# A gated mix of a state-space layer and linear attention: a new step list, and the last two output rows scaled and stored in halves

## Chip, cores and metric

The kernel runs on one core of a Trainium2 chip. The metric is the device time of one execution in microseconds. The profile is that of one further execution, taken by the hardware profiler; its span is the time from the first to the last instruction of the program on the core.

## What is computed

The input `x` has 2048 rows of 512 numbers. Branch `a` is a diagonal state-space layer (512 complex states, a recurrence over the rows), branch `b` is linear attention with 32 heads of 16, whose features are pairs of softmaxes. A gate of one number per row mixes them. Cut to what matters:

```python
g = sigmoid((x * gate_w).sum(-1, keepdims=True))
# a: h = Lam_bar * h + B_bar x_t, row by row;  y = 2 Re(C h) + x * Dskip
# b: q, k, v = x @ wqkv; phi = [softmax(+-(q|k) @ w_phi)]
#    kv = sum_s phi_k v;  z = sum_s phi_k;  o = phi_q kv / (phi_q z + 1e-6);  b = o @ wo
return g * a + (1 - g) * b
```

## The kernel before, in words

The 2048 rows are taken in 8 residues r of the row number modulo 8 and two halves each: 16 tiles of 128 rows. The recurrence over 2048 rows becomes one over 256 blocks (a scan on VectorE) and matmuls between residues. Nothing loops at run time: the order of all work on TensorE (PE), VectorE (DVE), ScalarE (ACT) and SyncE (SP) is a list written out by hand, the string `ORDER` (line 24). Each word names a step, a Python generator, and each time that the word occurs the step emits its next part. An engine executes its own parts in the order in which the list gives them. Behind `@` stand the numbers of the PSUM banks that the step takes; it has to wait until whoever had them has been read out. `:D` gives an evacuation or a scaling to VectorE instead of ScalarE, `:A` gives an output store to ScalarE's DMA queue instead of SyncE's. `F:28` puts 28 filler matmuls.

The steps that matter here, with the names of their tiles in the profile:

- `l8` to `l15` (`st_l`): SyncE loads one 128-row tile of x, transposed by the DMA, into `xT`; the tiles 0 to 7 are loaded ahead of the list. `NR`, `NI` load the real and imaginary part of B (512 KB each) into `Bn`.
- `k`, `v`, `q` (four matmuls of 512 columns each, line 475, and an evacuation): projections of one tile of x. `k9` needs x tile 9.
- `g`, `h`, `z`, `c`: the state-space branch. `y`: its output for one tile (`py`; two groups of four 512-column matmuls at line 717, then four 128-column matmuls with the diagonal of Dskip at line 722).
- `x`, `n`, `e`, `s` and, for the queries, `X1`-`X3`, `N1`-`N3`, `E1`-`E3`, `S1`-`S3`: softmax features of groups of four tiles. X and N are trees of maxima and minima on VectorE (line 511), then a subtraction; E is four exponentials on ScalarE; S is a tree of sums on VectorE, a logarithm on ScalarE, a difference on VectorE (line 553), an exponential on ScalarE, a multiplication on VectorE (line 559), and then four transposes by DMA, issued by SyncE (line 563), into `phT`. S1 gives the tiles of o4 to o7, S2 those of o8 to o11, S3 those of o12 to o15.
- `o0` to `o15` (`st_o`): attention output of one tile. Two matmul groups into `pn` (line 736), each followed by a logarithm and a copy to `nu`; then an exponential `rd`, a multiplication `on` (line 744), and a transpose into `oT`: by DMA from SyncE for the first twelve, by TensorE (`po`, line 753) for o12 to o15.
- `t0` to `t15` (`st_t`, line 761): four matmuls with `Wo` into the same `py` (line 765), then the scaling by the gate into `ot` (line 769 on ScalarE, 771 on VectorE), then one store of 128 rows of 512 numbers to the output (line 773).

The list ends with t15, t13 and t14.

Of the kernel before, what the change touches and what calls it, by code (L numbers as in the profile page):

```python
# [23 lines left out]
ORDER = """
NR F:28 NI B W1@0 W0@1 W0 W2@2 W1:D W3@3 W3 f1@4 W2:D f0@5 f2@6 f0 f1:D l10 V@0 F:4 V P f3@1 f3 f2:D F:4 P P k1@2 k1
l13 P2 k0@3 P2 U P2 P2 P2 P2 P4 k2@4 P3 P3 k3@5 P4 P4 k0 v0@0 i0 i2 U i0 i0 i1 i2 k4@7 i0:D i0 k2 i2 i2:D i2 U k3 k5@6
i1 v3@1 n0 x0 l9 i1 V2@2 i3 l12 x0 k4 v2@3 i3 i3 l14 i1 k5 n0 x0 n0 x0 i3 k7@4 n0 x0 U n0 i1 l11 k6@5 n1 x1 x1 n1 x1
n1 l8 R0 R1 x1 i3 k7 M v7@7 x1 n1 n1 k6:D L V2 v1@6 x2 n2 e0 v6@4 v5@5 v4@2 e0 x2 s0 v0 l15 n2 s0 n2 v2 s0 v1 R2 s0 v6
v3 n2 k10@0 k10 s0 k9@3 k9 C4 k13@6 gw D R3 s0 k12@4 e1 v7 s0 e1 s1 C6 k11@1 k11 x2 s1 k14@0 k8@3 k12 k14 k8 v4 k13
a0@71 a0 x2 s1 x2 s1 v5 g00@4 g00 g60@0 n2 x3 s1 g20@3 g60 s1 g10@2 g10 n3 e2 g30@6 g40@5 g10 s1 a1 x3 g20 n3 a1 x3 n3  # L30
x3 g41@4 n3 C3 e2 e2 e2 x3 g30 g40 g30 k15@0 k15 n3 e3 s2 x4 s2 x4 g01@2 g01 e3 e3 s2 g50@3 g11@5 g50 s2 s2 s2 n4 x4
n4 Q3 n4 s2 g50 g21@6 e3 s3 v8@0 g31@2 g11 Q2 g11 n4 g70@3 Q1 s3 C7 g21 g70 v9@5 g70 g70 z0 z0 g31 g31 Q0 w1@6 C0 a2
a2 a2 w0@3 s3 z0 v11@2 v9 g61@5 g41 R4 z0 w1 v8 z0 z0 g61 s3 w2@4 s3 s3 a2 x4 z0 z0 g51@6 g51 x4 w2 C2 s3 w3@0 g51 v11
n4 R5 w3 g71@5 g71 g71 g71 z1 z1 g02@4 g02 g42@6 a3 a3 z0 z0 g42 w0 e4 e4 z1 z1 z1 g62@2 g12@0 q1@5 C1 h50@4 C5 J1 e4
e4 z1 q2@6 q2 g12 g12 g22@3 g22 J0 h50 z1 z1 g62 q3@4 q3 J2 s4 z1 s4 q0@6 z1 s4 q0 q1 xA nA g32@0 J3 g32 g32 h60@3 J0
g52@2 g52 c4 h60 J2 c4 g52 h51@4 c2 s4 s4 g72@6 R7 g72 xA h10@5 nA g72 g72 c2 xA J3 nA h10 v10@0 v10 J1 s4 c5 h51 c5
R6 g23@3 v12@2 c4 c0 c0 g63@5 nA z2 z2 a3 a3 g03@4 xA g03 z2 z2 z2 z2 xA g23 z2 z2 g33@6 c5 v12 z2 z2 g13@0 g13 g63
g43@4 h32@3 g13 nA g43 h52@2 h52 g33 h32 h61@5 h61 h12@0 c0 g53@4 h12 g33 g53 s4 v14@3 c2 eA eA h42@2 h42 g73@6 g53 eA
eA g73 g73 q10@5 sA h11@0 h11 O h00@4 g73 sA v13@2 h00 v13 a4 z3 sA v15@6 z3 v15 h20@0 h01@4 h30@2 v14 h20 sA h30 z3
h31@6 z3 z3 sA a4 h01 h31 c6 c6 sA q13@3 q13 z3 a4 a4 Y Y h22@0 G q10 z3 z3 G q6@2 q6 h22 z3 z3 sA sA Y Y c1 c1 q9@4  # L40
q8@6 q5@7 h62@3 h41@5 c3 h41 c1 c3 c3 h13@0 h62 q11@2 h13 q11 q8 q12@1 c6 q12 h21@5 q5 h21 h02@2 c7 q4@6 q4 h53@3 h53
h23@1 h23 h33@0 h33 sA q9 h40@7 h40 sA q7@5 h43@6 h63@3 c7 h43 q7 c7 y4@0 y4 sA h63 sA h03@1 END h02 o0@4 o0 X1 N1
o1@7 o1 q14@6 X1 N1 h03 o0@5 X1 o1@2 o1 o1 o0 o0 q15@3 o2@4 o2 o2@7 o2 N1 q15 X1 N1 X1 N1 E1 E1 y2@1 y1@2 y1 E1 E1 q14
# [25 lines left out]
def kernel(  # L69
# [691 lines left out]
    def st_t(n):  # L761
        ti = order[n]
        py, oT = live["py", n], live["oT", n]
        for g in range(HG):
            MM(out=py[:], lhsT=oT[:, g, :], rhs=Wo[:, g, :], start=False, stop=(g == HG - 1))  # L765
        yield
        ot = pools["op"][1].tile([P, D], BF16, name="ot", bufs=14)
        if sel["eng"] == "act":
            nc.scalar.mul(out=ot[:], in_=py[:], mul=G[:, ti:ti + 1])  # L769
        else:  # L770
            VS(out=ot[:], in0=py[:], scalar1=G[:, ti:ti + 1], scalar2=None, op0=ALU.mult)
        yield
        sel["q"].dma_start(out=out_par[:, ti // 2, ti % 2, :], in_=ot[:])
        yield
# [73 lines left out]
```

## Time and profile before

| | |
|---|---|
| median of three runs | 155.21 us (154.76 to 155.4) |
| profiled execution's own time | 155.28 us |
| its span | 153.2 us |
| granted TensorE clock, mean | 0.995 |
| instructions | 3361 |

The profile's engines: PE is TensorE's matmuls, PEld its weight loads, DVE VectorE, ACT ScalarE, POOL GpSimd, SP SyncE; a q behind a name means the sequencer that issues DMAs or waits. A row of a timeline gives the start, the duration, the engine, the line, the operation, the tiles as out<-in, the shape and how many instructions are merged in it; in brackets the idle time of the engine before it and what ended it. Durations of neighbouring instructions of one engine overlap, so what one costs its engine is the distance from its start to the next one's start. "Chain" is the work that ended last, followed back from the end.

### The profile page before, as it was taken

The page shows a single profiled execution, that of the slowest core. Times are in us where ns is not written, and L with a number is a line of the kernel's source. Part 1 is how long each engine was busy: PE and PEld are TensorE (multiplying, and loading weights), DVE is VectorE, ACT ScalarE, POOL GpSimd, SP SyncE. Part 2 cuts the span into 40 slices and gives each one's busy share as a digit, 9 for nine tenths or more (in the row PEclk, how much of TensorE's full clock was granted, in tenths as well). Part 3 has the DMA queues.
Part 4 walks back from the last instruction along what each step waited for, and adds up shares of the span by engine and source line. Part 5 has one row for each costly group of instructions (what it writes and reads, how often), then busy time and mean ns, then how long its engine had stood idle before and what let it go on. Part 6 is the DMA issues. An engine that isn't in the chain of part 4 may idle for free.

```text
span 153.2 us, 3361 instructions
## 1 busy us (share of the span) xinstructions
PE 146.2 (95%) x1236; PEld 95.0 (62%) x1254; DVE 132.4 (86%) x303; ACT 129.2 (84%) x279; POOL 15.8 (10%) x43
## 2 busy tenths in 40 slices
...
GB/s 116 164 218 97 223 178 112 103 75 103 103 107 78 129 230 178 166 115 4 0 0 4 0 0 169 74 37 34 42 98 147 176 122 189 162 129 206 247 143 103
DMA packets 50848, 17.55 MB, mean 115 GB/s; under 512 B 44176, under 2 KB 50832, under 8 KB 50832
## 3 DMA queue, kind: packets, MB, share of 16 engines
...
q8 instruction: 10, 0.16, 0.5%
q0 software_dynamic: 160, 0.01, 0.2%
q14 instruction: 6, 0.05, 0.1%
...
## 4 chain that ended last, share of the span: by engine, by line
PE 78%; SPq 10%; DMA 7%; issue 1%; ACT 1%
PE pgq L601 18%; PE py L717 16%; PE pq L475 9%; PE py L765 8%; SPq L229 8%; PE pv L475 4%; PE ph L668 4%; PE pk L475 4%; DMA xT<-in_A_x_dram 4%; PE kvacc L578 3%; DMA phT<-EEq 3%; PE pn L736 3%; PE pgq L606 2%; PE py L722 2%; PE pgq L608 2%; SPq L284 1%
## 5 line engine op out<-in xcount | busy, mean ns | idle before, releaser
L601 PE MATMUL pgq<-xT,BT 128*128 128x256 bf16 x256 | 31.5, 272 | 0.0
L475 PEld LDWEIGHTS <-xT 128*128 128x128 bf16 x192 | 18.2, 98 | 18.3 <-DMA xT<-in_A_x_dram 0.7
L601 PEld LDWEIGHTS <-BT 128*128 128x128 bf16 x256 | 24.6, 98 | 4.1
L138 ACT ACTIVATE EEk<-EEk 128x1024 bf16<-128x1024 bf16 x20 | 20.4, 1080 | 0.0
L119 ACT CAST uv<-pgq 128x512 bf16<-128x512 f32 x28 | 15.9, 605 | 0.5 <-PE pgq L601 0.4
L475 PE MATMUL pv<-Wv,xT 128*128 128x512 bf16 x59 | 15.5, 379 | 0.3
L475 PE MATMUL pq<-Wq,xT 128*128 128x512 bf16 x60 | 15.4, 379 | 0.2
L765 PE MATMUL py<-Wo,oT 128*128 128x512 bf16 x62 | 15.3, 379 | 0.1
L475 PE MATMUL pk<-Wk,xT 128*128 128x512 bf16 x62 | 14.7, 379 | 0.3 <-DMA xT<-in_A_x_dram 0.2
L138 ACT ACTIVATE EEq<-EEq 128x1024 bf16<-128x1024 bf16 x12 | 11.7, 1042 | 0.3 <-DVE EEq L527 0.3
L769 ACT ACTIVATE ot<-py,G 128x512 bf16<-128x512 f32 x12 | 7.9, 686 | 4.5 <-PE py L765 4.3
L138 ACT ACTIVATE ld<-pn 128x16 f32<-128x16 f32 x32 | 6.1, 191 | 5.7 <-PE pn L736 4.6
L590 ACT ACTIVATE phT<-X,dgB 128x512 bf16<-128x512 bf16 x16 | 10.7, 725 | 0.0
L119 ACT CAST nu<-pn 128x256 bf16<-128x256 f32 x27 | 9.9, 380 | 0.0
L119 ACT CAST vx<-pv 128x512 bf16<-128x512 f32 x16 | 9.1, 604 | 0.4 <-PE pv L475 0.4
L548 DVE TENSOR_TENSOR EEk<-EEk,rck 128x4096 bf16<-128x4096 bf16 (+1 forms) x5 | 9.3, 1858 | 0.0
L744 DVE TENSOR_TENSOR on<-nu,rd 128x512 bf16<-128x512 bf16 x16 | 6.7, 421 | 2.8 <-ACT rd L138 1.6
L765 PEld LDWEIGHTS <-oT 128*128 128x128 bf16 x64 | 5.7, 97 | 5.3 <-DMA oT<-on 0.5
L119 ACT CAST Xq<-pq 128x512 bf16<-128x512 f32 x16 | 8.9, 608 | 0.0
L119 ACT CAST Xq<-pk 128x512 bf16<-128x512 f32 x15 | 8.6, 598 | 0.4 <-PE pk L475 0.4
L736 PEld LDWEIGHTS <-phT 128*128 128x128 bf16 x128 | 6.2, 97 | 3.8 <-DMA phT<-EEq 1.4
L511 DVE TENSOR_TENSOR smk<-smk 128x512 bf16<-128x512 bf16 (+4 forms) x18 | 8.1, 448 | 0.1
...
## 6 DMA issues: line engine op xcount, KB each, us to landing
...
out_dram<-ot ACTq DMA_DIRECT2D x8, 128.0 KB, 2.5
out_dram<-ot SPq DMA_DIRECT2D x8, 128.0 KB, 2.2
...
```

What stands on the lines that cost most here:

```text
L119: nc.scalar.copy(out=out_ap, in_=in_ap)
L138: ins = nc.scalar.activation(**kw)
L229: nc.sync.dma_start_transpose(out=xT[:, :, ti * P:(ti + 1) * P], in_=x_res[ti // 2, ti % 2])
L475: MM(out=pt[:], lhsT=xT[:, kt, ti * P:(ti + 1) * P], rhs=W[:, kt, :], start=(kt == 0), stop=(kt == KT - 1))
L511: VT(out=dst, in0=cur[:, :, :, 0:n, :], in1=cur[:, :, :, n:2 * n, :], op=op)
L548: VT(out=E5, in0=E5, in1=rc.to_broadcast([P, L, 2 * NB, Dh, 4]), op=ALU.mult)
L590: nc.scalar.mul(out=t_, in_=x_, mul=c_)
L601: MM(out=pg[:, h, :], lhsT=BT[:, kt, 2 * j + h, :], rhs=xT[:, kt, r * NC:(r + 1) * NC], start=(h == 0 and kt == 0), stop=(r % 2 == 0 and k ...
L717: MM(out=py[:], lhsT=hs(r, t, slice(a * P, (a + 1) * P)), rhs=C2B[t], start=(t == 0), stop=False)
L736: MM(out=pn[:, 4 * m:4 * m + 4, :].rearrange("p h e -> p (h e)"), lhsT=ph[:, 4 * hf + m, :], rhs=KVm[:, 4 * hf + m, :], start=(m == 0), st ...
L765: MM(out=py[:], lhsT=oT[:, g, :], rhs=Wo[:, g, :], start=False, stop=(g == HG - 1))
L769: nc.scalar.mul(out=ot[:], in_=py[:], mul=G[:, ti:ti + 1])
```

## The change

The list is replaced by another with the same 855 words. All steps do the same work, with other neighbours, other PSUM banks and other marks. At the head l14 and NI come ahead of l9 and NR; the K and V projections up to k15 come in another order. In the middle the state-space and attention steps are interleaved anew. At the end the last three rows are t15, t13, t14 again.

In `st_t`, for n of 14 and 15, the scaled row tile is made in two tiles `oh0` and `oh1` of 256 columns each, the left half scaled by ScalarE, the right half by VectorE, and each half is stored by itself, the left from ScalarE's queue, the right from SyncE's. The diff, with the list cut to its head, the stretch from S1 to E3 and its tail:

```diff
-NR F:28 NI B W1@0 W0@1 W0 W2@2 W1:D W3@3 W3 f1@4 W2:D f0@5 f2@6 f0 f1:D l10 V@0 F:4 V P f3@1 f3 f2:D F:4 P P k1@2 k1
-l13 P2 k0@3 P2 U P2 P2 P2 P2 P4 k2@4 P3 P3 k3@5 P4 P4 k0 v0@0 i0 i2 U i0 i0 i1 i2 k4@7 i0:D i0 k2 i2 i2:D i2 U k3 k5@6
-i1 v3@1 n0 x0 l9 i1 V2@2 i3 l12 x0 k4 v2@3 i3 i3 l14 i1 k5 n0 x0 n0 x0 i3 k7@4 n0 x0 U n0 i1 l11 k6@5 n1 x1 x1 n1 x1
...
-X2 y0@5 y0 o1 y4 X2 N2 X2 o0 o0 o3@4 o3 o3@7 o3 o1 o3 y2 X2 N2 o2 X2 N2 S1 S1 N2 S1 o3 S1 N2 S1 S1 o3 y5@3 o2 o2 S1 S1
-S1 y1 E2 E2 E2 E2 y9@6 G N3 y5 y5 y3@4 y2 X3 X3 N3 t1 G t1 N3 S1 N3 S2 y9 y9 S2 S2 S1 S1 S2 y3 y3 t3 y0 t0 t0 t2 t2
-y6@7 X3 t2:A o4@2 o4 o4@5 o4 o4 y6 y6 t3 X3 o4 X3 o4 S2 S2 t3 o5@1 o5 o5@2 o5 o5 y13@5 y13 o5 N3 o6@4 S2 o6 o6@1 o6 o6
-y12@2 o5 y7@4 y7 y12 o6 o6 t4 y7 S2 S2 t4:D S2 E3 E3 E3 E3 S2 o7@1 o7 t5 t5 S3 o7@0 o7 S3 o7 t6 S3 o7 S2 o7 y8@1 o8@3
...
-o11 y15 o13@4 o13:D o13@6 t6:A o13 o13 o11 o12 y10@1 o14@4 y15 o14:D o12@6 t9 o12:D t7:A t1 y10 y10 o13 o15@4 o15
-o15@6 t4:A t5 o15 o15 t8 o15 t12 t12 t12:A t10 o14@4 o14 o14 t10:D o13@6 t11 o15@2 o15 t10 o13:D t11 t11:A y13 t13 o14
-o14@1 t15 t15 t15 o14:D t14 t13 t13 t14 t14:A
+B l14 NI l9 NR F:28 W1@0 W1 W0@1 W0:D l8 W2@2 W2:D W3@3 W3 f1@4 f1:D f0@5 f0 f2@6 V@0 V P f2:D F:4 U P U l11 P2 P2 P2
+f3@1 P2 P2 P4 U f3 F:4 P4 P k1@2 P4 V2@3 V2 k1 l10 P2 P3 i1 P3 i2 k0@4 k0 i1 k2@5 k3@0 i3 i1 i1:D i1 v0@7 l13 k4@6 i2
+i2 l12 i3 i3 k3 v4@1 x0 k2 x0 i2 i0 x0 k4 n0 i0 i0 i0 R0 k5@2 k5 x0 n0 v1@3 i3:D i3 k6@4 x0 n0 x1 R1 n0 i2 x1 R2 i0 L
...
+E1 X2 N2 y0@4 y0 X2 G N2 X2 o1 X2 S1 N2 q15@1 S1 o3@7 o3 o3@5 o1 q15 o2 N2 o3 S1 o3 o3 S1 y1@3 N2 S1 S1 S1 X3 S1 E2 E2
+E2 y6 y6 o3 E2 S1 S1 y3 X3 N3 G X3 G y4@2 y4 y9@7 X3 y2@1 y9 y2 y2 y1 t2 y0 N3 y1 t1 S1 t0 t3 t0 t1 t3 X3 S2 y5@5 y5
+N3 t2 S2 S2 N3 S2 S1 o4@4 o4 o4@3 y13@6 o4 o4 o4 t3:A y4 o5@1 o5 o5@4 o5 o5 N3 S2 o5 y5 y7@3 o6@1 o6 t2 o6@4 o6:D y13
+o4 o6 y12@1 o5 S2 S2 o6 y12 y7 E3 E3 E3 o6 S2 S2 S2 o7@4 S2 t4 t5 S2 o7 o7@4 y7 t4:D E3 t0:A S3 S3 S3 t6 y12 o7 o7 o7
...
+t7:A o12@2 o12 o12@3 o12 o12 o12 y15 o13@7 o13 o13@2 o13:D o13 t6 y11 y10@3 y15 o14@7 o14 o12@2 o12:D y10 t5:A o15@7
+t8:A o15 o15@2 o15:D o15 o15 t12 o13 t12 t12 o14@7 o14 o14 o14 y10 t10 o15@2 t10 o13@1 o13 t11 o14@7 t11 o14 o15:D t11
+t10:A t15 t15 t15 t13 t13 t13 t14 t14 t14
...
             MM(out=py[:], lhsT=oT[:, g, :], rhs=Wo[:, g, :], start=False, stop=(g == HG - 1))
         yield
+        if n >= NTI - 2:
+            ha = [pools["op"][1].tile([P, D // 2], BF16, name=f"oh{c}", bufs=2) for c in range(2)]
+            nc.scalar.mul(out=ha[0][:], in_=py[:, 0:D // 2], mul=G[:, ti:ti + 1])
+            VS(out=ha[1][:], in0=py[:, D // 2:D], scalar1=G[:, ti:ti + 1], scalar2=None, op0=ALU.mult)
+            yield
+            for c, q in enumerate((nc.scalar, nc.sync)):
+                q.dma_start(out=out_par[:, ti // 2, ti % 2, c * (D // 2):(c + 1) * (D // 2)], in_=ha[c][:])
+            yield
+            return
         ot = pools["op"][1].tile([P, D], BF16, name="ot", bufs=14)
```

More of the change, by code (lines that the diff above doesn't have):

```diff
@@ L24 @@
 ORDER = """
-NR F:28 NI B W1@0 W0@1 W0 W2@2 W1:D W3@3 W3 f1@4 W2:D f0@5 f2@6 f0 f1:D l10 V@0 F:4 V P f3@1 f3 f2:D F:4 P P k1@2 k1
-l13 P2 k0@3 P2 U P2 P2 P2 P2 P4 k2@4 P3 P3 k3@5 P4 P4 k0 v0@0 i0 i2 U i0 i0 i1 i2 k4@7 i0:D i0 k2 i2 i2:D i2 U k3 k5@6
-i1 v3@1 n0 x0 l9 i1 V2@2 i3 l12 x0 k4 v2@3 i3 i3 l14 i1 k5 n0 x0 n0 x0 i3 k7@4 n0 x0 U n0 i1 l11 k6@5 n1 x1 x1 n1 x1
-n1 l8 R0 R1 x1 i3 k7 M v7@7 x1 n1 n1 k6:D L V2 v1@6 x2 n2 e0 v6@4 v5@5 v4@2 e0 x2 s0 v0 l15 n2 s0 n2 v2 s0 v1 R2 s0 v6
-v3 n2 k10@0 k10 s0 k9@3 k9 C4 k13@6 gw D R3 s0 k12@4 e1 v7 s0 e1 s1 C6 k11@1 k11 x2 s1 k14@0 k8@3 k12 k14 k8 v4 k13
@@ L30 @@
[L30 to L43, printed above, removed]
-X2 y0@5 y0 o1 y4 X2 N2 X2 o0 o0 o3@4 o3 o3@7 o3 o1 o3 y2 X2 N2 o2 X2 N2 S1 S1 N2 S1 o3 S1 N2 S1 S1 o3 y5@3 o2 o2 S1 S1
@@ L45 @@
-S1 y1 E2 E2 E2 E2 y9@6 G N3 y5 y5 y3@4 y2 X3 X3 N3 t1 G t1 N3 S1 N3 S2 y9 y9 S2 S2 S1 S1 S2 y3 y3 t3 y0 t0 t0 t2 t2
-y6@7 X3 t2:A o4@2 o4 o4@5 o4 o4 y6 y6 t3 X3 o4 X3 o4 S2 S2 t3 o5@1 o5 o5@2 o5 o5 y13@5 y13 o5 N3 o6@4 S2 o6 o6@1 o6 o6
-y12@2 o5 y7@4 y7 y12 o6 o6 t4 y7 S2 S2 t4:D S2 E3 E3 E3 E3 S2 o7@1 o7 t5 t5 S3 o7@0 o7 S3 o7 t6 S3 o7 S2 o7 y8@1 o8@3
-t6 o8 o8@0 o8 o8 S3 S3 y12 t0:A y11@7 o8 o8 o9@3 o9:D o9@0 o9:D S3 y8 y8 o9 o9 S3 S3 o9 o10@3 y11 o10 o10@0 y11 o10
-o10 S3 y14@3 S3 y14 t7 t7:D t8 y14 t8 y15@0 o11@4 S3 o11 o11@1 t9 o12@4 o11:D o11 S3 o10 o10 o12 o12@1 o12 o12 t9:D
@@ new lines @@
+i2 l12 i3 i3 k3 v4@1 x0 k2 x0 i2 i0 x0 k4 n0 i0 i0 i0 R0 k5@2 k5 x0 n0 v1@3 i3:D i3 k6@4 x0 n0 x1 R1 n0 i2 x1 R2 i0 L
+n0 x1 n1 n1 gw C0 l15 x1 R3 k6:D k7@0 k7 n1 U n1 x1 n1 e0 e0 k14@5 x2 n2 s0 v3@6 k14 x2 s0 v6@2 v6 k9@4 k9 v7@0 v0 v7
+v3 x2 v5@5 s0 n2 s0 s0 v5 n2 M D v2@2 s0 s0 v2 k8@4 e1 e1 s1 v1 k8 k11@7 k13@0 x2 k10@6 k10 s1 n2 k12@5 k12 a0@23 a0
+k13 s1 k11 g40@4 g40 x2 s1 s1 v4 s1 g00@6 g00 Q2 g60@5 g60 g10@0 n2 x3 e2 g20@7 g20 g10 g10 g30@4 Q0 e2 e2 n3 e2 s1 a1
+a1 g01@1 x3 k15@6 n3 x3 n3 g01 x3 k15 g30 g30 g11@5 C3 n3 C7 x3 n3 s2 s2 g31@7 s2 g50@0 g11 x4 e3 e3 s2 g50 n4 g50
@@ new lines @@
+g41@1 C5 s2 s2 g11 g70@6 e3 e3 g21@4 g21 g70 g61@0 R4 g70 x4 v8@5 n4 g70 x4 g61 v8 s2 a2 a2 a2 Q3 a2 g31 g31 g41 Q1
+w2@4 w2 R5 x4 s3 s3 n4 w3@6 C2 C1 s3 x4 R6 w1@0 g02@5 w1 g02 z0 s3 C4 s3 w3 g51@7 g51 w0@1 w0 z0 n4 g51 z0 R7 g71@4
+g52@0 g71 s3 g71 g71 z0 z0 z0 n4 C6 J3 e4 g22@5 g22 g12@6 g12 g12 z0 z0 q1@1 e4 s3 g32@7 z1 z1 z0 z0 g42@4 g42 g32
+h50@5 g32 e4 e4 z1 z1 z1 q3@6 z1 h10@4 q3 q2@7 g52 h50 z1 z1 g62@5 h10 g52 q2 g62 q0@4 J1 g72@6 s4 z1 z1 s4 q1 q0 xA
+nA g72 s4 c5 xA g72 g72 z2 nA J2 h60@0 h60 v11@7 v11 nA z2 g03@5 g03 nA J0 J0 xA v10@1 z2 z2 z2 z2 v10 g23@4 g43@6 c3
@@ new lines @@
+v9@7 a3 J3 xA J1 g23 c3 c3 h51@5 J2 z2 z2 g33@0 h51 c2 v9 c4 c2 c5 a3 a3 c4 s4 a3 g43 z2 z2 xA c5 g13@1 s4 s4 g13 g13
+nA v12@4 v12 h52@7 h32@5 h32 h52 h61@6 h61 g33 g33 h11@1 h11 g63@4 s4 eA eA g53@5 g53 g53 g73@0 g63 c4 v14@7 eA eA
+h42@6 h42 h12@1 h12 g73 h00@5 sA h31@4 c2 sA v13@6 g73 g73 z3 z3 v13 v15@1 h01@0 v14 c0 v15 c0 q14@6 h00 sA h01 a4 z3
+z3 z3 sA sA a4 c1 z3 q14 a4 c0 a4 h62@7 h02@1 h02 Y q12@5 c1 q7@0 q7 z3 sA sA z3 q6@6 q6 Y G Y Y z3 z3 q12 c1 h22@1
+q5@2 sA q4@3 h31 q10@0 h30@6 h62 c6 h22 sA sA h41@5 h41 q5 h20@4 h20 h13@2 h13 q4 c6 c6 h53@7 sA h21@3 q8@1 h33@5 c7
@@ new lines @@
+c7 c7 h30 q11@4 h40@2 h21 h53 sA h33 h43@6 O h23@5 q9@3 h43 h40 h63@7 h23 q10 q8 h63 h03@0 END o0@1 y3@6 X1 o0 N1 o0@2
+X1 N1 X1 o0 N1 o1@5 X1 q9 N1 y3 h03 q11 X1 o2@1 o0 o2 o2@7 o2 o2 o1 N1 o0 o0 o1@2 q13@3 q13 X2 o2 o1 o1 y6@0 E1 E1 E1
+E1 X2 N2 y0@4 y0 X2 G N2 X2 o1 X2 S1 N2 q15@1 S1 o3@7 o3 o3@5 o1 q15 o2 N2 o3 S1 o3 o3 S1 y1@3 N2 S1 S1 S1 X3 S1 E2 E2
+E2 y6 y6 o3 E2 S1 S1 y3 X3 N3 G X3 G y4@2 y4 y9@7 X3 y2@1 y9 y2 y2 y1 t2 y0 N3 y1 t1 S1 t0 t3 t0 t1 t3 X3 S2 y5@5 y5
+N3 t2 S2 S2 N3 S2 S1 o4@4 o4 o4@3 y13@6 o4 o4 o4 t3:A y4 o5@1 o5 o5@4 o5 o5 N3 S2 o5 y5 y7@3 o6@1 o6 t2 o6@4 o6:D y13
```

2 lines of the change are left out of this document (added).

## The prediction

> **What bounds the kernel now.** First the page: the engines' shares, and the chain that ended last by engine.
>
> ```profile
> PE 146.2 (95%) x1236; PEld 95.0 (62%) x1254; DVE 132.4 (86%) x303; ACT 129.2 (84%) x279; POOL 15.8 (10%) x43
> PE 78%; SPq 10%; DMA 7%; issue 1%; ACT 1%
> ```
>
> TensorE is busy 95% of the span of 153.2 us and makes 78% of the chain. Shares are means over stages, so next come the windows (columns: stretch, length, PE, PEld, DVE, ACT, POOL).
>
> ```profile
> 40.00:50.00 10.00, 9.90 (x121) 8.04 (x122) 9.93 (x21) 9.42 (x18) 0.00 (x0) 1.00 0.52 98
> 80.00:90.00 10.00, 9.95 (x100) 6.31 (x100) 9.91 (x25) 9.33 (x22) 0.00 (x0) 1.00 0.01 2
> 100.00:110.00 10.00, 9.95 (x69) 5.18 (x69) 9.97 (x23) 8.23 (x23) 0.00 (x0) 1.00 0.20 40
> 110.00:120.00 10.00, 9.95 (x76) 5.33 (x75) 9.60 (x21) 8.44 (x18) 0.00 (x0) 1.00 0.78 119
> 120.00:130.00 10.00, 9.71 (x71) 4.96 (x72) 7.59 (x12) 9.17 (x26) 0.00 (x0) 1.00 0.80 159
> 130.00:140.00 10.00, 9.95 (x90) 5.50 (x90) 5.44 (x11) 5.27 (x21) 0.00 (x0) 1.00 0.90 157
> ```
>
> PE and VectorE are full together up to 110; only behind that does VectorE fall to 5.4 of 10, while the DMA share rises to 0.9. A list that only reorders the same matmuls can win at the head (before PE runs full), in PE's few waits, and behind the last matmul. The waits are in the chain and in PE's timeline:
>
> ```profile
> 17.02 5.82 DMA xT<-in_A_x_dram
> 22.89 5.35 PE pk L475 x24
> 21.70 1.03 PE L475 MATMUL pk<-Wk,xT 128*128 128x512 bf16 x4
> 116.71 4.37 DMA phT<-EEq
> 119.92 1.03 PE L717 MATMUL py<-C2i,Bn 128*128 128x512 bf16 x3
> 121.13 0.43 PE L736 MATMUL pn<-KVm,phT 128*128 128x68 bf16 x8 [0.18 <-DMA phT<-EEq]
> 35.36 0.90 PE pgq L601 x8
> ```
>
> Four 512-column matmuls take 0.86 us from start to start (21.70 is followed, PE free, by 22.56; the chain's usual piece is 0.86 to 0.90). So k9, the group at 22.89, waited 0.33 us for x9, and o6 at 121.13 waited 0.35 us (119.92 + 0.86 = 120.78; one matmul of four is missing in that row) for the third transposed tile of S1. These two are the places to look at.
>
> **The head: worth 0.** SyncE now issues l14, NI, l9, NR, l8 instead of NR, NI, l10, l13, l9. x9 moves from the fifth of these places to the third, two places of about 1.3 us, and PE reaches k9 earlier by four groups less one (v2, v7, v5, k10 go behind it, k14 ahead): 3 x 0.86 = 2.6 us. Supply and demand move alike, so between 0 and 0.33 us of the wait goes. I count nothing at the end for either, because VectorE is full in the same stretch and the next wait, at o6, hangs on VectorE: what PE gains early it waits there. The changed :D marks put, on balance, two copies of o steps (0.38 us each, by a row below) and the scalings of t7 and t10 (0.69 each) from VectorE on ScalarE, 2.1 us, all in the tail, where ScalarE has 4.7 of 10 us free (window 130 to 140): cost 0, and if that cover were gone, at most the 2.1 us.
>
> **S1 and o6: +0.22 us.** The rows around S1's last multiplication (L559), the transposes that it releases and the store between them:
>
> ```profile
> 111.09 0.28 DVE L553 TENSOR_TENSOR dlq<-lgq 128x128 f32<-128x128 f32 x1
> 111.29 0.42 DVE L744 TENSOR_TENSOR on<-nu,rd 128x512 bf16<-128x512 bf16 x1
> 111.75 1.22 DVE L559 TENSOR_TENSOR EEq<-EEq,rhoq 128x2048 bf16<-128x2048 bf16 x1
> 112.97 0.68 DVE L511 TENSOR_TENSOR mnq<-Xq 128x1024 bf16<-128x1024 bf16 x1
> 113.57 0.68 DVE L511 TENSOR_TENSOR mxq<-Xq 128x1024 bf16<-128x1024 bf16 x1
> 113.03 6.66 SPq L563 DMA_TRANSPOSE phT<-EEq  x4
> 117.50 0.36 ACTq L773 DMA_DIRECT2D out_dram<-ot  x1
> ```
>
> Walking both lists up to S1's multiplication, VectorE's work ahead of it is the same but for one instruction more: X3's first maximum, 0.60 us from start to start (112.97 to 113.57), which stands where o2's normalisation stood. That one (0.34 to 0.4 us) moves ahead of the subtraction L553 and delays it; behind L553, X3's step fills 0.60 us where 0.46 passed (111.29 to 111.75, an idle end in it). Sum: 0.36 + 0.14 = 0.5 us later, so the four transposes start at about 113.5. Against that, t2's store, which ScalarE issued at 117.50 between the third and the fourth, is now SyncE's and comes behind the fourth.
>
> ```profile
> DMA packets 5353, 1.44 MB, mean 166 GB/s; under 512 B 5224, under 2 KB 5352, under 8 KB 5352
> q8 instruction: 1, 0.02, 3.7%
> phT<-EEq SPq DMA_TRANSPOSE x2, 4.4
> phT<-EEq SPq DMA_TRANSPOSE x12, 3.3
> ```
>
> In the window 113 to 121.7 the DMAs moved 166 GB/s, so the store's 0.13 MB are worth up to 0.8 us to what is queued with them. The third tile's landing therefore lies between 0.5 us later and about 0.5 us earlier than 121.09; I take it as unmoved, by the row itself. PE's work ahead of o6 becomes 0.22 us smaller (y13's second half and y9's diagonal part, 0.86 + 0.22, go; y7's first half, 0.86, comes). With o6 fixed by the tile, that 0.22 us lies behind it: the last matmul ends 0.22 us later than 149.17. The same stretch has one instruction block in it (second and third row, window 113.4 to 116: 3.7% of 16 engines for 2.6 us, 1.5 us of one engine), and the two transposes issued then needed 4.4 us against 3.3 in the median of twelve. If the blocks are PE's (it has the most instructions by far), the new list has as many of them behind it at the same time within about 0.2 us, so the block will meet the same transposes again.
>
> The Trainium skill ("Runtime: NRT & Kernel Launch", section "Instruction fetch mechanics") says that crossing a 16 KiB block of instructions costs one bump of a DMA tail and is mostly hidden; by that, counting such packets in a list would be worth nothing. The 4.4 against 3.3 us speak against it for transposes under way, though a busy queue could do the same.
>
> From S1 on, SyncE's transposes are back to back in both lists in the same groups (4, 3, 4, 3, 4, 2), and o8, o12, o13 and o15 have the same PE work ahead of them within 0.22 us. I add nothing there.
>
> **The last two rows: -0.54 us.** The end, in the timeline, the chain, the groups by form and the DMA view of the last 5 us:
>
> ```profile
> 147.28 1.89 PE L765 MATMUL py<-Wo,oT 128*128 128x512 bf16 x8
> 149.23 0.27 issue
> 149.50 0.69 ACT ot L769
> 150.22 0.34 ACTq L773 DMA_DIRECT2D out_dram<-ot  x1
> L119 ACT CAST nu<-pn 128x256 bf16<-128x256 f32 x27 | 9.9, 380 | 0.0
> L119 ACT CAST Xq<-pq 128x512 bf16<-128x512 f32 x16 | 8.9, 608 | 0.0
> L771 DVE TENSOR_SCALAR ot<-py,G 128x512 bf16<-128x512 f32 x4 | 3.0, 750 | 4.2 <-PE py L765 4.1
> L121 DVE CAST nu<-pn 128x256 bf16<-128x256 f32 x5 | 2.0, 423 | 2.6 <-ACT ld L138 2.6
> L121 DVE CAST Xq<-pk 128x512 bf16<-128x512 f32 x1 | 0.7, 684 | 0.0
> out_dram<-ot SPq DMA_DIRECT2D x2, 128.0 KB, 1.9
> out_dram<-ot ACTq DMA_DIRECT2D x1, 128.0 KB, 2.0
> ```
>
> Before: the last matmul ends at 149.17; ScalarE still scales t15 and t13, begins t14 at 149.50, ends it at 150.19, issues at 150.22; 2.0 us to landing, 0.98 us more to the span's end: 4.03 us behind the last matmul. After: PE runs t15, t13, t14, each 0.86 apart, and ScalarE's t13 (0.69) is done before t14's matmuls end. A half costs ScalarE 0.69 x 380/608 = 0.43 and VectorE, free there, 0.75 x 423/684 = 0.46 us, side by side. Then 0.02 + 0.46 + 0.03 + 2.0 + 0.98 = 3.49 us, 0.54 less. t15's store on ScalarE's queue puts 0.34 us ahead of t13's scaling; ScalarE has t15's half (0.43), the store and t13 done before t14 all the same. Bounds: 0.04 if halves need 2.5 us to land (the page's median for ScalarE's stores), 0.64 if 1.9.
>
> [...]
>
> **The sum.** 153.2 + 0.22 - 0.54 = 152.9 us of span. The profiled run took 155.28, 2.08 more than its span; the median of the three, 155.21, is 0.07 lower. Forecast: 155.28 - 0.32 - 0.07 = 154.9 us.
>
> **Rivals.**
> *Transposes early.* The store out of the way lets the third tile land before PE needs it. PE is at o6 by 120.78 - 0.22 - up to 0.33 = 120.23. Gain: 121.13 - 120.23 = 0.90, less the 0.22, plus the tail's 0.54: 1.2 us, 154.0 us. For it: 0.8 us of store traffic gone. Against: VectorE's 0.5 us.
>
> *Transposes late (slower).* S1's multiplication ends 0.5 us later, and the instruction block, about 1 us behind the first transpose before, now comes with its start; its 1.5 us of one engine then delay all four. Place: o6 and, through E3 and S3's transposes, o12 on. Price: up to 0.5 + 0.9 (the block's remainder) = 1.4 at o6; 0.22 + 1.4 - 0.54 = +1.1 us, 156.2 us. The kernel becomes slower once the third tile lands after 121.09 + 0.32 = 121.4, and slower by over 0.5% after 122.2. For it: 4.4 us landings with one block. Against: the block's bytes are the same.
>
> *A wait in the middle.* PE and VectorE are full from 20 to 110, so one evacuation placed too late stops PE. Before, PE waited there only a few tenths in all; one misplaced 0.6 us evacuation with its queue costs 0.5 to 1.5 us: about 155.9.
>
> *The halves do nothing.* If both halves' stores land in 2.5 us, the tail gives 0.04: 155.3 us.
>
> **Chances.** Forecast, with the halves that do nothing: 0.52. Transposes early: 0.22. Transposes late: 0.16. A wait in the middle: 0.10, half of it over the bound. A measurement of this kernel tells about 0.5% (0.8 us) from no change, so by cases: faster 0.24 (the early case and 0.02 of the forecast's), slower 0.22 (the late case, 0.05 of the middle, 0.01 of the forecast's), same 0.54. The range reaches from the early case to just past the late one: 153.7 to 156.3 us.
>
> **What would show it.** S1's multiplication near 112.25 instead of 111.75, with X3's maximum before it. A wait of some tenths at o6 for phT, longer than before because PE comes earlier. k9 with little or no wait. Behind the last matmul about 3.5 us, two halves side by side. The prediction is wrong if PE waits over half a microsecond anywhere between 24 and 110, if the third tile lands outside 120.6 to 121.6, or if the half stores take longer than whole ones.

## The result, and the profile after

| | before | after |
|---|---|---|
| median of four runs each | 154.99 us (154.61 to 155.4) | 157.34 us (156.36 to 158.44) |
| ratio | | 1.0139, 95% interval 1.0097 to 1.0181 |
| profiled execution, its span | 155.28 us, 153.2 us | 157.63 us, 155.5 us |
| end of PE's last matmul row | 149.17 us | 151.57 us |
| from there to the span's end | 4.0 us | 4.0 us |

The changed kernel is 1.4% slower, where a gain of 0.3 us was forecast, and lies outside the forecast's range. The end behind the last matmul hardly shrank (by 0.07 us), and the last matmul ends 2.4 us later. The page of the changed kernel shows hardly any of it: PE's share of the span is 95% as before, and only in the chain by line have the landings of transposes grown: `phT` has 6% where it had 3%, and `oT`, with 5%, is new.

```profile
PE 147.0 (95%) x1235; PEld 96.4 (62%) x1254; DVE 130.4 (84%) x301; ACT 130.4 (84%) x283; POOL 14.8 (10%) x43
PE pgq L601 18%; PE py L717 12%; PE pk L475 9%; PE pq L475 9%; PE pv L475 8%; DMA phT<-EEq 6%; PE py L765 5%; DMA oT<-on 5%; PE ph L668 4%; PE kvacc L578 3%; PE spin L821 2%; PE pgq L606 2%; PE pn L736 2%; PE pgq L608 2%; PE pf L431 1%; PE py L722 1%
```

The windows say where. Up to 130 PE is as full as before; in the next ten microseconds it has 8.92 instead of 9.95, while the DMA engines are as busy as before (0.91) and move less (130 GB/s against 157):

```profile
120.00:130.00 10.00, 9.89 (x82) 5.46 (x83) 7.30 (x13) 9.31 (x25) 0.00 (x0) 1.00 0.83 174
130.00:140.00 10.00, 8.92 (x73) 4.79 (x71) 3.91 (x8) 4.74 (x20) 0.00 (x0) 1.00 0.91 130
```

PE's timeline of the changed kernel has the waits themselves; o6, which waited before, is the row at 120.48:

```profile
119.61 1.03 PE L717 MATMUL py<-C2r,HM 128*128 128x512 bf16 x4
120.48 0.42 PE L736 MATMUL pn<-KVm,phT 128*128 128x68 bf16 x8
...
133.96 0.29 PE L736 MATMUL pn<-KVm,phT 128*128 128x68 bf16 x4
134.76 1.04 PE L765 MATMUL py<-Wo,oT 128*128 128x512 bf16 x4 [0.51 <-DMA oT<-on]
...
136.85 0.29 PE L736 MATMUL pn<-KVm,phT 128*128 128x68 bf16 x4
137.66 1.04 PE L765 MATMUL py<-Wo,oT 128*128 128x512 bf16 x4 [0.52 <-DMA oT<-on]
...
139.65 1.02 PE L717 MATMUL py<-C2i,Bn 128*128 128x512 bf16 x4
141.84 0.43 PE L736 MATMUL pn<-KVm,phT 128*128 128x68 bf16 x8 [1.16 <-DMA phT<-EEq]
...
146.96 0.39 PE L753 MATMUL po<-ident,on 128*128 128x128 bf16 x4
147.50 0.40 PE L753 MATMUL po<-ident,on 128*128 128x128 bf16 x4 [0.16 <-DVE on L744]
```

A wait is read from start to start: four 68-column matmuls take 0.13 us, four of 512 columns 0.86, four of 128 columns 0.22 (the brackets are smaller, since a row's duration reaches past the next start). o6 comes at 120.48, 0.65 us earlier than before, and waits for nothing. Then PE waits 134.76 - 133.96 - 0.13 = 0.67 us at t7 and 0.68 at t9 for the DMA transposes into `oT`, 1.33 at o13 for S3's second tile, and 0.32 at a transpose of its own: 3.0 us in all, where the kernel before had 0.35 at o6 and 0.13 elsewhere in the tail. So a lead of 0.65 us at 120 became a loss of 2.4 us at the end. The waits are larger than the loss, since a part of them only gives that lead back.

What stands among those transposes are output stores. ScalarE's queue in the changed kernel, below it SyncE's transposes, after and before, and for the changed kernel the time of the 12 into `phT` from issue to landing as minimum, median and maximum:

```profile
118.70 0.36 ACTq L782 DMA_DIRECT2D out_dram<-ot  x1
124.52 0.40 ACTq L782 DMA_DIRECT2D out_dram<-ot  x1
127.51 0.34 ACTq L782 DMA_DIRECT2D out_dram<-ot  x1
137.85 0.34 ACTq L782 DMA_DIRECT2D out_dram<-ot  x1
138.23 0.53 ACTq L782 DMA_DIRECT2D out_dram<-ot  x1
```

```profile
124.05 6.18 SPq L563 DMA_TRANSPOSE phT<-EEq  x4
130.33 5.15 SPq L758 DMA_TRANSPOSE oT<-on  x3
135.58 6.04 SPq L563 DMA_TRANSPOSE phT<-EEq  x4
```

```profile
124.61 5.39 SPq L563 DMA_TRANSPOSE phT<-EEq  x4
130.10 4.62 SPq L758 DMA_TRANSPOSE oT<-on  x3
134.83 5.39 SPq L563 DMA_TRANSPOSE phT<-EEq  x4
```

```profile
DMA to landing us min/median/max: 3.2/4.1/5.5
```

The stores are t3, t0, t4, t1 and t7. The list before put two on ScalarE's queue before 140 (t2 at 117.50, t0 at 129.70). The delay adds up in SyncE's queue, where the transposes stand back to back: from the first of S2 to the end of the last of S3 their issue takes 17.6 us (124.05 to 141.62), before 15.6 (124.61 to 140.22). The DMA view of the stretch in which S3's transposes are under way shows both sides, before and after (q1 is SyncE's queue, q10 ScalarE's):

```profile
q1 hardware_dynamic: 3715, 0.92, 86.4%
phT<-EEq SPq DMA_TRANSPOSE x4, 3.2
```

```profile
q1 hardware_dynamic: 1523, 0.38, 82.7%
q10 hardware_dynamic: 93, 0.10, 20.0%
phT<-EEq SPq DMA_TRANSPOSE x3, 4.2
```

Before (134.5 to 140.2 us) nothing but SyncE's transposes moves there, and they land 3.2 us after their issue; after (137.5 to 140.2) two stores take 20% of the engines' time and the three transposes issued there need 4.2.

The two halves, last, do not stand side by side. Timeline of the end, and the waits view (total, times, longest):

```profile
151.61 0.47 ACT L769 ACTIVATE oh<-py,G 128x256 bf16<-128x256 f32 x1
152.12 0.48 DVE L770 TENSOR_SCALAR oh<-py,G 128x256 bf16<-128x256 f32 x1 [1.24 <-ACT oh L769]
```

```profile
DVE oh L770 <- ACT oh L769: 3.5, 2, 2.3
```

VectorE's half starts at 152.12, when ScalarE's has ended, though VectorE had been idle for 1.24 us, the last 0.5 of them for nothing but ScalarE's half (from 151.61). Both halves read the same PSUM tile `py`, and the program has a semaphore between them.

### The profile page after: what moved, and what is told of

It is laid out like the page before. It is cut to its first block, busy times and chain, and to the rows that moved or that the text cites. A ratio compares the mean times of both kernels' runs of the same rounds, so it can differ in the third digit from the quotient of the medians.

```text
span 155.5 us, 3362 instructions
## 1 busy us (share of the span) xinstructions
PE 147.0 (95%) x1235; PEld 96.4 (62%) x1254; DVE 130.4 (84%) x301; ACT 130.4 (84%) x283; POOL 14.8 (10%) x43
## 3 DMA queue, kind: packets, MB, share of 16 engines
HBM read 2.64 MB, written 2.10 MB: 30 GB/s over the span
## 4 chain that ended last, share of the span: by engine, by line
PE 83%; DMA 11%; ACT 2%; DVE 1%; issue 1%
PE pgq L601 18%; PE py L717 12%; PE pk L475 9%; PE pq L475 9%; PE pv L475 8%; DMA phT<-EEq 6%; PE py L765 5%; DMA oT<-on 5%; PE ph L668 4%; PE kvacc L578 3%; PE spin L821 2%; PE pgq L606 2%; PE pn L736 2%; PE pgq L608 2%; PE pf L431 1%; PE py L722 1%
## 5 line engine op out<-in xcount | busy, mean ns | idle before, releaser
L601 PE MATMUL pgq<-xT,BT 128*128 128x256 bf16 x256 | 30.9, 272 | 0.1
L119 ACT CAST nu<-pn 128x256 bf16<-128x256 f32 x28 | 10.5, 384 | 0.0
L736 PE MATMUL pn<-KVm,phT 128*128 128x68 bf16 x128 | 7.4, 194 | 1.2 <-DMA phT<-EEq 1.2
```

The source lines that it names most:

```text
L119: nc.scalar.copy(out=out_ap, in_=in_ap)
L601: MM(out=pg[:, h, :], lhsT=BT[:, kt, 2 * j + h, :], rhs=xT[:, kt, r * NC:(r + 1) * NC], start=(h == 0 and kt == 0), stop=(r % 2 == 0 and k ...
L736: MM(out=pn[:, 4 * m:4 * m + 4, :].rearrange("p h e -> p (h e)"), lhsT=ph[:, 4 * hf + m, :], rhs=KVm[:, 4 * hf + m, :], start=(m == 0), st ...
```

## The experiments

Four questions, with a theory and a rival each. **A**: the stores that the new list puts among the DMA transposes make them land late. **B**: the instruction block that comes at 131 to 133 us does it. **Tail**: do the halves, or the order t13 before t14, set what lies behind the last matmul? **Head**: does PE's wait at k9 count at the end? Each ratio is that to the kernel before on the same chip, with its 95% interval.

### Stores moved out of the new list

```diff
 t4:D E3
-t0:A
 S3 S3 S3 t6 y12 o7 o7 o7 o7 t5 t6 y8@2
-t4:A
 o8@4
...
 o11 o11 y15@5
-t1:A t7:A
 o12@2
...
 o13:D o13 t6
+t0 t4 t1 t7
 y11
```

This is the list of the run with four stores late: they are issued by SyncE behind its last DMA transpose. The runs with one pair late move t0 and t4, or t1 and t7.

> The changed kernel with four stores moved (t0, t4, t1, t7): from ScalarE's queue, where they were issued at 124.5, 127.5, 137.9 and 138.2 us among the transposes of S2 and S3, to SyncE's queue behind the last DMA transpose. Nothing else changes. Theory A (stores slow the transposes that are under way): the waits of TensorE behind 128 us (0.67 at t7, 0.68 at t9, 1.33 at o13) fall to some 0.5 us in all, and the time falls by 2.0 to 2.4 us, to the time of the kernel before or a little under it. Theory B (the block of instructions at 131.6 us meets another transpose than before, stores are innocent): the waits and the time stay within 0.5 us of the changed kernel.

> Only t0's and t4's stores (issued at 124.5 and 127.5 us, among S2's transposes) are moved behind the last transpose. Theory A: the fourth transpose of S2 lands in about 3.7 us instead of 5.5, the two waits at t7 and t9 (1.35 us) fall to about 0.4, and about 1 us is gained. Theory B: under 0.3 us.

> Only t1's and t7's stores (issued at 137.9 and 138.2 us, among S3's transposes) are moved behind the last transpose. Theory A: S3's second transpose lands in about 3.3 us instead of 4.8, the wait of 1.33 us at o13 falls under 0.4, and about 1 us is gained. Theory B: under 0.3 us.

| late | ratio | PE's waits in the tail |
|---|---|---|
| t0, t4, t1, t7 | 1.0056 (1.0026 to 1.0086) | 0.49 at o12, 1.30 at o15 |
| t0, t4 | 1.008 (1.005 to 1.0111) | 0.30, 0.18, 0.25, 0.67, 0.21 |
| t1, t7 | 1.0052 (1.0016 to 1.0087) | 0.35, 0.35, 0.16, 0.68 |

The waits at t7, t9 and o13 go with all four. The landings show what each pair does: with t0 and t4 late S2's four transposes land 3.3 to 3.4 us after their issue (3.8 to 5.5 in the changed kernel) and S3's after 3.9 to 4.3; with t1 and t7 late S3's land after 3.2 to 3.3 (3.4 to 4.8) and the last of S2 still after 4.9. The ratios of the pairs are less sharp: on this chip the changed list with whole rows had 1.010 (1.0055 to 1.0145), whose interval overlaps all three. And with t1 and t7 late the waits at t7 and t9 fell to 0.35 and 0, although they lie ahead of these two stores; that part of the difference is not theirs.

With four late a new wait comes. Timeline of that kernel, ScalarE's next store and what stands behind it:

```profile
143.34 1.40 ACTq L782 DMA_DIRECT2D out_dram<-ot  x2
144.79 0.18 ACT L138 ACTIVATE ld<-pn 128x16 f32<-128x16 f32 x1 [2.39 <-DMA out_dram<-ot]
145.28 0.29 PE L736 MATMUL pn<-KVm,phT 128*128 128x68 bf16 x4 [1.14 <-ACT nu L119]
```

ScalarE came to the stores of t5 and t8, and its arithmetic stood for 2.39 us: t5's store was issued when an earlier transfer that uses the same semaphore had landed, a transpose of SyncE's (143.31), t8's when an earlier store of SyncE's had (144.38), and the two issues themselves took 0.38 and 0.34. Behind them on ScalarE stood o15's logarithm and copy, for which PE waits. So these two were made late as well (whole rows at the end, so that only the list is tried):

```diff
 o13:D o13 t6 t0 t4 t1 t7
+t5 t8
 y11 y10@3 y15 o14@7 o14 o12@2 o12:D y10
-t5:A
 o15@7
-t8:A
 o15
```

> The new list with six stores (t0, t4, t1, t7, t5, t8) on SyncE's queue behind the last DMA transpose, so that ScalarE issues no store between 119 and 146 us, and whole rows at the end. In the run with four stores moved, ScalarE's t5 and t8 still stood ahead of o15's copies, 1.4 us in its queue, and TensorE waited 1.30 us there. Theory A: that wait goes too, TensorE waits under 1 us in all behind 128 us, and the time is that of the kernel before or up to 1 us under it. Theory B: no faster than with four moved (1.0056 of the kernel before).

The changed kernel itself was run beside it on the same chip:

> The changed kernel itself, beside the others on one chip: 1.010 to 1.018 of the kernel before.

Six late: 1.0032 (1.0001 to 1.0063). The change: 1.0186 (1.0147 to 1.0226).

In the tail of the kernel with six late, PE's timeline has one wait left:

```profile
139.02 0.43 PE L736 MATMUL pn<-KVm,phT 128*128 128x68 bf16 x8 [0.50 <-DMA phT<-EEq]
```

### The same stores put into the list before

```diff
 S2 S2 t4:D S2 E3 E3 E3 E3
+t0:A
 S2 o7@1
...
 t6
+t4:A
 o8 o8@0
...
 y12
-t0:A
 y11@7
...
 o11:D o11
+t1:A t7:A
 S3 o10
```

(t1 and t7 leave their old places, and so does t4. t1's store was SyncE's before and is now ScalarE's.)

> The list before the change, with only four stores brought forward to the places that they have in the new list, on ScalarE's queue: t0 behind E3's exponentials, t4 behind t6's scaling, t1 and t7 behind o11's exponential. Theory A (stores among the transposes delay them, and a store on ScalarE's queue holds what stands behind it): waits of over 1 us in all appear for TensorE between 126 and 145 us, and the kernel becomes slower by 1.0 to 2.2 us (0.7 to 1.4%). Theory B (the block of instructions, or something else in the new list): within 0.4 us of the kernel before.

1.0139 (1.0104 to 1.0173), the same loss as the change. PE's waits in it:

```profile
131.52 0.30 PE L736 MATMUL pn<-KVm,phT 128*128 128x68 bf16 x4 [0.16 <-DMA phT<-EEq]
142.12 0.30 PE L736 MATMUL pn<-KVm,phT 128*128 128x68 bf16 x4 [0.95 <-DMA phT<-EEq]
144.41 0.43 PE L736 MATMUL pn<-KVm,phT 128*128 128x68 bf16 x8 [0.46 <-DMA phT<-EEq]
```

Together 2.1 us, all ended by landings of `phT`; the last matmul row ends at 151.04, 1.9 us later than before. Only four words moved, and the instruction block comes at 132.6 us, where it came before (132.4). Theory A holds both ways: taking the stores out of the new list takes nearly all of the loss away (1.0032 is left, 1.0019 in a second run of it below), putting them into the old one makes it. B is not needed for it. What is not told apart: S2's last transpose is still under way when the block comes (131.6 in the changed kernel), so a part of its 5.5 us may be the block's. And that the stores act through the shared DMA engines is argued from the DMA view above.

### Halves and the order of the last three rows

The changed list with whole rows, and the list before with halves (in both only `st_t` differs):

> The new list with the last two rows scaled whole and stored once, as before the change. In the changed kernel VectorE's half began only when ScalarE's had ended (152.12 behind 151.61 + 0.47), 3.93 us from the end of the last matmul to the end of the span. If halves one behind the other gain nothing: behind the last matmul 0.02 + 0.69 + 0.03 + 2.0 + 1.0 = 3.7 us, and the time changes by -0.2 us (within noise). If the halves are worth the 0.54 us of the prediction: 0.5 us slower.

> The list before the change with the last two rows scaled and stored in halves. If the halves wait for each other: within 0.3 us of the kernel before. If they are worth the 0.54 us of the prediction: 0.4 to 0.6 us faster.

Whole rows in the changed list: 1.010 (1.0055 to 1.0145). Halves in the list before: 1.0106 (1.0068 to 1.0143), slower than either theory had it, with a wait of 1.6 us that neither kernel had:

```profile
149.14 0.48 DVE L770 TENSOR_SCALAR oh<-py,G 128x256 bf16<-128x256 f32 x1 [2.33 <-ACT oh L769]
149.54 0.41 DVE L121 COPY oT<-po 128x512 bf16<-128x512 bf16 x1
150.01 1.04 PE L765 MATMUL py<-Wo,oT 128*128 128x512 bf16 x4 [1.42 <-DVE oT L121]
```

VectorE stands 2.33 us at t15's half, first for t15's matmuls and in the last 0.5 us for ScalarE's half (148.63 to 149.10), and the copy that t14's matmuls need is queued behind it. Next the order alone, in the list before with whole rows:

```diff
-t15 t15 t15 o14:D t14 t13 t13 t14 t14:A
+t15 t13 t13 t15 t15 o14:D t14 t14 t14:A
```

> The list before with one thing changed: at its end t13's scaling and store come ahead of t14's matmuls and t15's store, so that ScalarE has done t15 and t13 when t14's matmuls end. Whole rows. Theory 'the tail gain of the change is the order, not the halves': the time from the last matmul's end to the last landing falls from 3.2 to 2.8 us, ratio 0.996 to 0.999. If the halves made the gain: ratio 1.000, and 3.2 us as before.

> As the run with the tail's order alone, and also the two ScalarE stores that stand among S1's and S2's transposes in the list before (t2, t0) on SyncE's queue behind its last DMA transpose. Theory 'stores among transposes delay them': the wait of 0.35 us at o6 goes or shrinks to 0.1, ratio 0.993 to 0.997. If stores don't matter: the wait at o6 stays at 0.3 to 0.4 us and the ratio is that of the tail's order alone.

0.9964 (0.9925 to 1.0004), and with t2 and t0 late as well 0.9962 (0.9936 to 0.9988). At S1 the second bears theory A out: with t2's store out of the way the third tile landed 3.23 us after its issue, against 4.26 with the order alone, and o6, which still waited 0.23 us there, waits for nothing. At the end nothing is left of it, since PE then waits 0.98 us for a transpose into `oT` (more on it in the last section). The traces give the tail in two parts, the second from the last store's landing to the end of the program:

| kernel | rows 14 and 15, order | last matmul row's end to last landing | landing to span's end | sum |
|---|---|---|---|---|
| before | whole, t14 before t13's scaling | 3.06 | 0.98 | 4.04 |
| old list, order alone | whole, t13 first | 2.64 | 0.98 | 3.62 |
| changed list, whole rows | whole, t13 first | 2.62 | 0.98 | 3.60 |
| changed | halves, t13 first | 2.70 | 1.26 | 3.96 |
| old list with halves | halves, behind the wait of 1.6 us | 2.71 | 1.27 | 3.98 |

(The expectations count from the last matmul's start plus the time of its columns, 0.16 us ahead of the row's end.) The order is worth 0.42 us in the old list and 0.44 in the new. The halves take 0.36 of it back: their landing is 0.08 later, and the end behind the landing is 0.29 longer. The second part can be followed in SyncE's waits at the end of the program. Records of the trace (start, duration, the semaphores that the wait names; ordinary output, not a view), the changed kernel with whole rows and with halves:

```
whole  155.008 0.028 (107,110)  155.743 0.028 (108,101)  155.802 0.028 (109,118)
halves 153.010 1.289 (102,100)  154.336 0.028 (104,114)  154.397 0.028 (105,113)
       154.461 0.028 (106,112)  154.523 0.027 (107,111)  154.582 0.028 (108,110)  154.644 0.028 (109,101)
```

SyncE waits for the stores' semaphores in a fixed order, 0.06 us apart. With whole rows the last store to land (at 155.73) is in the last pair but one; with halves two stores more have moved the last one (154.28) into the first pair, and six waits come behind it that could have been done meanwhile. If so, halves for one row only, with one store more, move it on by one place, into the last pair:

```diff
-        if n >= NTI - 2:
+        if n == NTI - 2:
```

> The changed list with only t14 in halves; t15 is scaled and stored whole. With both rows in halves the program's end comes 1.27 us behind the last landing, with whole rows 0.98 us; SyncE waits at the end for the stores' semaphores one after the other in a fixed order, 0.06 us each, and with both rows in halves the last store's semaphore stands first in that order, with whole rows last but one. Theory 'the halves' price is the place of the last store's semaphore in that order': one store less moves the last one to the last place, the end comes 0.9 to 1.0 us behind the landing, and from the end of PE's last row to the span's end it takes 3.6 to 3.7 us instead of 3.96. Theory 'halves themselves lengthen the end': 1.25 us or more behind the landing, 3.95 in all. The ratio stays at 1.010 to 1.018 either way, since the waits among the transposes are untouched.

> The list before with t13 ahead of t14, and t14 alone in halves. With whole rows this list had 3.62 us from the end of PE's last row to the span's end and a ratio of 0.996. By the theory of the semaphore's place: landing 2.70 behind PE's end and 0.9 to 1.3 more, depending on the place that the last store gets; t15 is whole, so VectorE's copy for t14's matmuls isn't held up as with both rows in halves. Expected 3.6 to 4.0 us, ratio 0.995 to 0.999: no better than whole rows. If halves save time in a free tail: 3.4 us or less, ratio 0.994 or below.

The last store was then in the last pair in both, landing to end took 0.91 and 0.92 us, and the sum 3.61 and 3.63: the semaphore's place was the price. The ratios are 1.013 (1.0087 to 1.0173) in the changed list, whose waits for the transposes stay, and 0.9967 (0.9937 to 0.9997) in the old one with t13 first. With whole rows that one had 0.9964 above: half rows are worth nothing here. ScalarE's half, then VectorE's, are 0.47 + 0.04 + 0.48 us against 0.69 for a whole row, and the smaller store lands only 0.2 to 0.3 us faster (1.7 against 1.9 to 2.0). Halves in two PSUM tiles of their own, which might need no semaphore between them, were not tried.

### The head

```diff
-B l14 NI l9 NR F:28
+B l14 l9 NI NR F:28
```

> The changed list with whole rows, six ScalarE stores (t0, t4, t1, t7, t5, t8) moved to SyncE's queue behind the last DMA transpose, and l9 ahead of NI at the head. In the run with the six stores late, PE waited 1.23 us at k9 for x9. Theory 'the head counts': that wait goes and everything behind it comes 0.8 to 1.2 us earlier, ratio to the kernel before 0.994 to 0.998. Theory 'the head is worth 0' (VectorE, full up to 110, gives the gain back at o6): the wait at k9 goes, one of 0.5 us or more appears at o6 or ahead of it, and the time stays within 0.3 us of the six-late kernel, ratio 1.001 to 1.005.

> The same six-late list with l14 and NI ahead of l9 as in the change, but with the last two rows in halves. Theory 'halves one behind the other': VectorE's half starts only when ScalarE's has ended, the half stores land 0.2 to 0.3 us sooner than whole ones, from the last matmul's end to the last landing 2.8 to 2.9 us, ratio within 0.002 of the six-late kernel with whole rows (1.003). Prediction's theory 'halves side by side': 0.3 us or more sooner, ratio 1.001 or below. It is also the control for the l9 run, since only the tail differs.

These two, 0.9979 (0.9947 to 1.0012) and 1.0047 (1.0012 to 1.0082), differ in l9 and in the halves. So the parts were run singly on one chip, and l9 alone within the change:

> The six-late list with l9 ahead of NI, last two rows in halves. Beside the same list with whole rows (f3, same chip) only the tail differs. Theory 'the halves gain next to nothing because VectorE's half waits for ScalarE's': ratio within 0.002 of f3, last matmul's end to last landing 2.7 to 2.9 us. Theory 'the halves cost time' (as the run of six late stores with halves stood 0.7% above the one with l9 and whole rows): ratio 0.004 or more above f3, with a wait of PE in the tail that f3 hasn't.

> The six-late list with l14 and NI ahead of l9 as in the change, whole rows: the control for f3 on the same chip. Ratio near 1.003.

> The same with l9 ahead of NI. Theory 'the wait at k9 counts': the wait there is under 0.5 us where f2 has 1 us or more, and the ratio is 0.004 to 0.008 below f2's. Theory 'the head is worth 0': ratio within 0.002 of f2's, with what PE gains at k9 lost again at o6 or o13.

> The changed kernel with one thing altered: l9 ahead of NI. All ScalarE stores stay among the transposes. If the head counts by itself: k9's wait goes and the time is 0.6 to 1.0 us below the changed kernel's, ratio 1.008 to 1.013. If the transposes in the tail set the time (SyncE's queue then has the same landings whatever PE does before): waits at t7, t9 and o13 grow by what was gained at k9, ratio 1.013 to 1.019 as for the changed kernel.

| list | rows | ratio |
|---|---|---|
| six late, as in the change (f2) | whole | 1.0019 (0.9993 to 1.0046) |
| six late, l9 ahead of NI (f3) | whole | 0.9995 (0.9973 to 1.0018) |
| six late, l9 ahead of NI (f1) | halves | 1.001 (0.9984 to 1.0035) |
| changed, l9 ahead of NI (f4) | halves | 1.0139 (1.0099 to 1.018) |

PE's timeline at the head, first f2, then f3:

```profile
20.78 1.04 PE L475 MATMUL pk<-Wk,xT 128*128 128x512 bf16 x4 [0.90 <-DMA xT<-in_A_x_dram]
21.66 2.75 PE L475 MATMUL pv<-Wv,xT 128*128 128x512 bf16 x12
24.25 1.03 PE L475 MATMUL pk<-Wk,xT 128*128 128x512 bf16 x4
```

```profile
20.78 2.75 PE L475 MATMUL pv<-Wv,xT 128*128 128x512 bf16 x12
24.04 1.25 PE L475 MATMUL pk<-Wk,xT 128*128 128x512 bf16 x5 [0.51 <-DMA xT<-in_A_x_dram]
```

With l9 first the wait at k9 goes and a smaller one follows at the next tile; PE is 0.2 us ahead at 24, and in these two profiles the last matmul row ends at 149.46 against 149.41. Over all runs l9 ahead of NI is worth more: twelve each on one chip have means of 156.13 (f2) and 155.66 (f3), a difference of 0.46 us, 0.1 to 0.8 at 95%. The halves beside it (f1 against f3) cost 0.35 us, 0.1 to 0.6.

Within the change no gain shows (1.0139, as the change had on another chip): the waits at t7, t9, o13 and at the last transposes are then 0.64, 0.74, 1.45 and 0.55. But the wait at k9 itself does reach the end. Two profiles of the changed kernel differ in it, none in the one and 1.4 us in the other (the run beside the six-late kernel): VectorE begins the same subtraction, of a maximum from the queries' features (L521), at 100.10 and 101.19, S1's multiplication at 111.75 and 112.84, and the last matmul row ends at 151.57 and 152.72; the runs took 157.63 and 158.77 us.

## Why the prediction was wrong

The direction was missed by one step: **"From S1 on, SyncE's transposes are back to back in both lists in the same groups (4, 3, 4, 3, 4, 2) ... I add nothing there."** The groups are right, and so is PE's work between them. But the step looked at SyncE's queue alone. Four stores (t0, t4, t1, t7) moved forward on ScalarE's queue in among these transposes (one of them, t0, had stood right behind S2's), and the two queues share the DMA engines. The prediction had the price beside it: a store of 0.13 MB is "worth up to 0.8 us to what is queued with them". Four of them by that figure are up to 3.2 us; brought forward in the old list they made the last matmul row end 1.9 us later, and in the change, where they are not all that differs, it ends 2.4 us later. The one store that was taken out by itself between two lists, t2 at S1, was worth 1.0 us to the third transpose's landing (4.26 against 3.23 us). The prediction counted the price once, for t2, and not for the four. It also looked at the work ahead of o8, o12, o13 and o15 alone, and not at t7 and t9, which wait for the same queue: t9 has four 512-column matmuls, 0.86 us, less ahead of it in the new list, and almost half of the waits came there. The Trainium skill ("DMA: Bandwidth & Descriptors", section "Issuing engines are not separate DMA queues") says that DMAs of different issuing engines run on the same 16 engines and interleave; the 3.2 against 4.2 us agree.

**The late transposes** among the rivals had the sign and the kind of wait, and named o12 on as one place. Its cause, a later S1 multiplication that meets the instruction block, was not the one at work: the multiplication was not later. Its 156.2 us (155.21 + 1.08 makes 156.3) was 1.1 too low.

**S1 and o6: +0.22.** Wrong by 0.5 us in its first term, S1's multiplication, and by 1.3 us in the landing that it took as unmoved. Two rows of VectorE in the changed kernel:

```profile
111.14 0.70 DVE L511 TENSOR_TENSOR mxq<-Xq 128x1024 bf16<-128x1024 bf16 x1
111.75 1.23 DVE L559 TENSOR_TENSOR EEq<-EEq,rhoq 128x2048 bf16<-128x2048 bf16 x1
```

X3's maximum does stand ahead of S1's multiplication, as read from the lists, and fills 0.61 us where 0.46 passed. But the multiplication starts at 111.75, as before: VectorE had come to this stretch 0.35 us ahead (the subtraction at L521 at 100.10 instead of 100.45), so that L553 began 0.15 us earlier (110.94) and not 0.36 later. With the store of t2 out of the way the third tile landed at 119.75 instead of 121.09 and was there when PE came, as the rival of early transposes had it: o6 at 120.48, where that rival said 120.23. Its gain was made and lost again behind.

**The head: worth 0.** That supply and demand move alike held only roughly, and "what PE gains early it waits there" failed. In the changed kernel's profile x9 landed 3.1 us earlier than before (19.73 against 22.84) and PE came 2.3 us earlier, so the whole wait of 0.33 us was gone, and VectorE was 0.35 us ahead at 100. In f2's x9 landed at 20.74, and PE waited 1.1 us; of the 1.0 us between the two, 0.3 is the issue of l14 ahead of it (2.0 us instead of 1.7, where 1.3 was counted) and 0.7 the landing itself. As the two profiles of the changed kernel show, such a wait is not absorbed on the way: at L521 VectorE was 0.35 us ahead of before in the one and 0.74 behind in the other (100.10, 101.19, before 100.45). That 0 lies between the two is luck; why x9's landing varies stays open.

**The last two rows: -0.54.** Measured, from the last matmul to the span's end, -0.07. The step that failed is "side by side": the two halves go one behind the other. The duration of a half was right (0.47 and 0.48 us against 0.43 and 0.46), and the whole gain, 0.44 us, is that of t13 ahead of t14, which the prediction had named in passing; 0.36 us of it goes to the halves and the order of the final waits. A row that the prediction shows already has VectorE waiting for ScalarE on one PSUM tile (`nu` behind `ld`, 2.6 us); it was read for its duration alone. The Trainium skill ("PSUM — Partial Sum Buffer", section "PSUM bank collisions raise a hardware error") says that two engines must not access one bank at once, reads included, and that a dependency is put between them. The trace agrees: both times VectorE's half starts when ScalarE's has ended (150.40 and 152.12 behind 149.89 + 0.47 and 151.61 + 0.47), so that ScalarE's half is the last 0.5 us of the waits of 2.3 and 1.2 us.

**ScalarE's 2.1 us more, at no cost**, was not tried by itself. The wait of 1.3 us with four stores late shows one case in which ScalarE's idle time in the tail was no cover: a store in its queue waited for a semaphore.

The kernel that beats both is the list before with t13 scaled and stored ahead of t14: ratios of 0.9964, 0.9962 and 0.9967 in its three forms (order alone, two stores late, t14 in halves), with the intervals above, of which two end below 1, by little. It is worth about 0.5 us, and 0.42 us of that can be followed in the tail of its trace.
